# A linear-attention and MLP kernel on one core: a fixed issue order on TensorE, a 5/4 token layout, kv per head, and batches 0 to 2 turned on TensorE

## The chip, the cores and the metric

The kernel runs on one core of a Trainium2 chip. The metric is device time in microseconds (us) of one execution, as the median of several. The profile's span of a run is about 1.7 us shorter than the time that is reported for the same run.

Profile lines name the engines: PE is TensorE (matmuls), PEld its loads of the stationary operand, DVE VectorE, ACT ScalarE, POOL GpSimd, and SP (SPq) SyncE, whose queue issues DMA. L176 is line 176 of that run's kernel. To turn a tile is to transpose it. q turns, kv and o are the small matmuls of the attention; PSUM is the memory that matmuls write to. A hole is a stretch in which TensorE has nothing to run, and a cold matmul one that runs at about half rate.

Executions of the kernel before vary: 342 to 350 us over all chips used here. Some are marked slow: over 1.5% above the fastest of the same kernel on that chip. Ratios below are the mean time of one kernel's fast runs over that of the other's of the same rounds, so not quite the ratio of the medians that are quoted.

## The reference

Eight batches, eight heads, 576 tokens, head width 64. Everything after the attention works on rows of 512 (8 heads of 64).

```python
kv  = einsum('bhsd,bhse->bhde', k, v)              # 64 x 64 per head
out = einsum('bhsd,bhde->bhse', q, kv)
rms = sqrt(mean(out * out, axis=-1) + 1e-6)
x   = (out / rms * g_norm)                          # heads side by side: (8, 576, 512)
xn  = (x - mean(x)) / sqrt(var(x) + 1e-6) * g_ln    # layer norm over 512
res = x + relu(xn @ w_ch1) @ w_ch2                  # 512 -> 2048 -> 512
```

Inputs and output are float32; the kernels load q, k, v and the weights as bfloat16.

## The kernel before

Tokens are taken as 128 partitions of 4 tokens (512), and the other 64 tokens of a batch as a remainder. Two batches' remainders make one tile of 128 rows. So there are 32 main tiles and 4 remainder tiles, and nine MLP blocks of four tiles. MLP 1 is 64 matmuls of 512 columns a block, MLP 2 also 64.

```python
def load_batch(b):                       # casts f32 -> bf16; issued by GpSimd
    for src, main, rem in ((q, q_m, q_r), (k, k_m, k_rem[...]), (v, v_m, v_rem[...])):
        nc.gpsimd.dma_start(main, src[b, :, :S_MAIN, :].rearrange("h (p j) d -> p h j d", j=J))
        nc.gpsimd.dma_start(rem, src[b, :, S_MAIN:, :].rearrange("h p d -> p h d"))

def permuted(b, t, tag):                 # [p, h, j, d] -> [p, j, h, d], for q and for k
    eng = nc.vector if b in PERM_DVE else nc.gpsimd          # PERM_DVE = (0,)
    eng.tensor_copy(t_p.rearrange("p j h d -> p h j d"), t)

def transpose_q(b, q_m, q_r):            # the DMA branch is the one taken for all batches
    q_p = permuted(b, q_m, "qp")
    nc.sync.dma_start_transpose(q_t..., q_p...)
    nc.sync.dma_start_transpose(q_tr, q_r...)

def kv_product(b, k_m, v_m):             # two heads at a time: 128 x 128, 20 matmuls a batch
    k_p = permuted(b, k_m, "kp")
    for hp in range(HP):
        for j in range(J):
            nc.tensor.matmul(kv_ps[:, hp, :], lhsT=k_p[:, j, hs, :]..., rhs=v_m[:, hs, j, :], ...)
        nc.tensor.matmul(...)            # the remainder
    # ... the two diagonal 64 x 64 blocks are copied to kv_pack

def attn_tile(mms, x_blk, mv_blk, xT_blk, ts, xt_pe):
    # o_ps = q_t . kv_pack (4 matmuls); ScalarE: sq, rms; VectorE: ss, inv, y, x, stats, mv,
    xc = work.tile([128, Dm], bf16, tag="xc")                # 3 buffers
    nc.vector.tensor_scalar(xc, x2, mv_blk[:, ts, 0:1], None, op0=ALU.subtract)
    if xt_pe: ...                        # turned on TensorE: batch 0 only
    else:     nc.sync.dma_start_transpose(xT_blk[:, :, ts * 128:(ts + 1) * 128], xc)

# order of issue: attention of batch b+1, then the MLP of batch b
blk0 = attn(0, l0)
for b in range(B):
    if b + 1 < B:
        if b + 2 < B: loads[b + 2] = load_batch(b + 2)
        blks[b + 1] = attn(b + 1, loads.pop(b + 1))
    if b == B - 1: moe(rem_blk, store_rem)
    moe(blks.pop(b), store_main(b))
```

w1 is multiplied by g_ln after it is loaded, by ScalarE and VectorE in turn. The framework's scheduler chooses the order on each engine.

Of the kernel before, what the change touches and what calls it, by code (L numbers as in the profile page):

```python
# [14 lines left out]
def kernel(  # L15
# [11 lines left out]
    nc = tc.nc  # L27
    f32 = mybir.dt.float32
# [8 lines left out]
    assert Dm == 512 and Dh % 512 == 0 and S == 576 and D == 64  # L37
# [3 lines left out]
    J = 4  # L41
    S_MAIN = 128 * J
    S_REM = S - S_MAIN
    EPS = 1e-6
    PERM_DVE = (0,)
    QT_PE = ()
    XT_PE = (0,)

    consts = ctx.enter_context(tc.tile_pool(name="consts", bufs=1))
    kv_in = ctx.enter_context(tc.tile_pool(name="kv_in", bufs=2))  # L50
    qt_pool = ctx.enter_context(tc.tile_pool(name="qt_pool", bufs=2))
# [4 lines left out]
    ps_kv = ctx.enter_context(tc.psum_pool(name="ps_kv", bufs=1))  # L56
    ps_out = ctx.enter_context(tc.psum_pool(name="ps_out", bufs=2))
    ps_tp = ctx.enter_context(tc.psum_pool(name="ps_tp", bufs=1))
    ps1 = ctx.enter_context(tc.psum_pool(name="ps1", bufs=2))
    ps2 = ctx.enter_context(tc.psum_pool(name="ps2", bufs=2))  # L60


    g_norm_sb = consts.tile([128, 1, D], f32)
    nc.scalar.dma_start(
        g_norm_sb,
        bass.AP(tensor=g_norm.tensor, offset=g_norm.offset,
                ap=[[0, 128], [0, 1], list(g_norm.ap[0])]),
    )
    g_ln_col = consts.tile([128, nK, 1], f32)
    g_ln_r = moe_g_ln.rearrange("(ko p) -> p ko", p=128)  # L70
    nc.scalar.dma_start(
        g_ln_col,
        bass.AP(tensor=g_ln_r.tensor, offset=g_ln_r.offset,
                ap=[list(x) for x in g_ln_r.ap] + [[1, 1]]))
    eps_sb = consts.tile([128, 1], f32)
    nc.vector.memset(eps_sb, float(EPS))
    identity = consts.tile([128, 128], bf16)

    w1_sb = consts.tile([128, nK, Dh], bf16)
    w2_sb = consts.tile([128, nDe, Dm], bf16)  # L80

    NB_REM = 2
    k_rem = [consts.tile([128, H, D], bf16, name=f"k_rem{i}") for i in range(NB_REM)]
    v_rem = [consts.tile([128, H, D], bf16, name=f"v_rem{i}") for i in range(NB_REM)]
    kv_pack = [consts.tile([128, HP, 128], bf16, name=f"kv_pack{i}") for i in range(3)]

    def load_batch(b):
        q_m = kv_in.tile([128, H, J, D], bf16, tag="qm")
        k_m = kv_in.tile([128, H, J, D], bf16, tag="km")
        v_m = kv_in.tile([128, H, J, D], bf16, tag="vm")  # L90
        q_r = kv_in.tile([S_REM, H, D], bf16, tag="qr")
        for src, main, rem in ((q, q_m, q_r), (k, k_m, k_rem[b % NB_REM][:S_REM]),
                               (v, v_m, v_rem[b % NB_REM][:S_REM])):
            nc.gpsimd.dma_start(  # L94
                main, src[b, :, :S_MAIN, :].rearrange("h (p j) d -> p h j d", j=J))
            nc.gpsimd.dma_start(
                rem, src[b, :, S_MAIN:, :].rearrange("h p d -> p h d"))
        return q_m, q_r, k_m, v_m

    def load_w1():  # L100
        for c in range(4):
            n = Dh // 4
            sl = slice(c * n, (c + 1) * n)
            nc.gpsimd.dma_start(
                w1_sb[:, :, sl], moe_w_ch1[:, sl].rearrange("(ko p) n -> p ko n", p=128))
            for kk in range(nK):
                if kk % 2 == 0:
                    nc.scalar.mul(w1_sb[:, kk, sl], w1_sb[:, kk, sl], g_ln_col[:, kk, :])  # L108
                else:
                    nc.vector.tensor_scalar(w1_sb[:, kk, sl], w1_sb[:, kk, sl],  # L110
                                            g_ln_col[:, kk, :], None, op0=ALU.mult)

    def load_w2():
        for c in range(4):
            n = nDe // 4
            nc.gpsimd.dma_start(
                w2_sb[:, c * n:(c + 1) * n, :],
                moe_w_ch2[c * n * 128:(c + 1) * n * 128, :].rearrange(
                    "(ko p) n -> p ko n", p=128))

    def permuted(b, t, tag):
        t_p = kv_in.tile([128, J, H, D], bf16, tag=tag)
        eng = nc.vector if b in PERM_DVE else nc.gpsimd
        eng.tensor_copy(t_p.rearrange("p j h d -> p h j d"), t)  # L124
        return t_p

    def transpose_q(b, q_m, q_r):
        q_t = qt_pool.tile([128, J, HP, 128], bf16, tag="qt")
        q_tr = qt_pool.tile([128, HP, S_REM], bf16, tag="qtr", bufs=3)
        q_p = permuted(b, q_m, "qp")  # L130
        if b in QT_PE:
            for j in range(J):
                tp = ps_tp.tile([128, HP, 128], bf16, tag="tp")
                for hp in range(HP):
                    nc.tensor.transpose(tp[:, hp, :], 
                                        q_p[:, j, 2 * hp:2 * hp + 2, :].rearrange("p h d -> p (h d)"),
                                        identity)
                nc.vector.tensor_copy(q_t[:, j], tp)
            tp = ps_tp.tile([128, HP, 128], bf16, tag="tp")
            for hp in range(HP):  # L140
                nc.tensor.transpose(
                    tp[:, hp, :S_REM],
                    q_r[:, 2 * hp:2 * hp + 2, :].rearrange("p h d -> p (h d)"),
                    identity[:S_REM, :S_REM])
            nc.vector.tensor_copy(q_tr, tp[:, :, :S_REM])
        else:
            nc.sync.dma_start_transpose(
                q_t.rearrange("p j hp t -> p (j hp) t"), q_p.rearrange("p j h d -> p (j h d)"))
            nc.sync.dma_start_transpose(q_tr, q_r.rearrange("p h d -> p (h d)"))
        return q_t, q_tr  # L150

    def kv_product(b, k_m, v_m):
        kvp = kv_pack[b % 3]
        k_p = permuted(b, k_m, "kp")
        kv_ps = ps_kv.tile([128, HP, 128], f32, tag="kvps")
        for hp in range(HP):
            hs = slice(2 * hp, 2 * hp + 2)
            for j in range(J):
                nc.tensor.matmul(kv_ps[:, hp, :], lhsT=k_p[:, j, hs, :].rearrange("p h d -> p (h d)"),  # L159
                                 rhs=v_m[:, hs, j, :],  # L160
                                 start=(j == 0), stop=False)
            nc.tensor.matmul(kv_ps[:, hp, :],  # L162
                             lhsT=k_rem[b % NB_REM][:, hs, :].rearrange("p h d -> p (h d)"),
                             rhs=v_rem[b % NB_REM][:, hs, :].rearrange("p h d -> p (h d)"),
                             start=False, stop=True)
        nc.vector.tensor_copy(kvp[:D, :, :D], kv_ps[:D, :, :D])  # L166
        nc.vector.tensor_copy(kvp[D:, :, D:], kv_ps[D:, :, D:])
        return kvp

    def attn_tile(mms, x_blk, mv_blk, xT_blk, ts, xt_pe):  # L170

        o_ps = ps_out.tile([128, H, D], f32, tag="ops")
# [15 lines left out]
        x3 = x_blk[:, ts].rearrange("p (h d) -> p h d", h=H)  # L188
        nc.vector.tensor_mul(x3, y, g_norm_sb.to_broadcast([128, H, D]))  # L189
        x2 = x_blk[:, ts]  # L190
# [3 lines left out]
        xc = work.tile([128, Dm], bf16, tag="xc")  # L194
        nc.vector.tensor_scalar(xc, x2, mv_blk[:, ts, 0:1], None, op0=ALU.subtract)  # L195
        if xt_pe:
            tp = ps_tp.tile([128, HP, 128], bf16, tag="tp")
            for kk in range(nK):
                nc.tensor.transpose(tp[:, kk, :], xc[:, kk * 128:(kk + 1) * 128], identity)  # L199
            nc.vector.tensor_copy(xT_blk[:, :, ts * 128:(ts + 1) * 128], tp)  # L200
        else:
            nc.sync.dma_start_transpose(xT_blk[:, :, ts * 128:(ts + 1) * 128], xc)
# [7 lines left out]
    def rstd_of(blk, lo=0, hi=4):  # L210
        rstd = work.tile([128, 4, 1], f32, tag="rstd")
        nc.scalar.activation(rstd[:, lo:hi], blk[1][:, lo:hi, 1:2], func=AF.Sqrt, bias=eps_sb)
        nc.vector.reciprocal(rstd[:, lo:hi], rstd[:, lo:hi])
        return rstd

    def moe(blk, store):
        x_blk, mv_blk, xT_blk = blk
        rstd = rstd_of(blk)
        m1 = m1pool.tile([128, nDe, 512], bf16, tag="m1")
        for de in range(nDe):  # L220
            p1 = ps1.tile([128, 512], f32, tag="p1")
            for kk in range(nK):
                nc.tensor.matmul(p1, lhsT=w1_sb[:, kk, de * 128:(de + 1) * 128],  # L223
                                 rhs=xT_blk[:, kk, :], start=(kk == 0), stop=(kk == nK - 1))
            nc.scalar.activation(m1[:, de, :], p1, func=AF.Relu)
        for ts in range(4):
            p2 = ps2.tile([128, Dm], f32, tag="p2")
            for de in range(nDe):
                nc.tensor.matmul(p2, lhsT=m1[:, de, ts * 128:(ts + 1) * 128],  # L229
                                 rhs=w2_sb[:, de, :], start=(de == 0), stop=(de == nDe - 1))  # L230
# [88 lines left out]
```

## Time and profile before

Median 348.03 us (346.2 to 349.99, 3 runs). The execution that was profiled took 350.6 us and is marked slow, so the stages and holes below are those of a slow execution; no fast one of this kernel was profiled. The stages are cut at what TensorE does: its first MLP matmul, the end of MLP 1 of batch 0, the first matmul of MLP 1 of batch 2, and its last matmul.

| stage of the kernel before | us |
|---|---|
| start: to the first MLP matmul | 48.30 |
| MLP 1 of batch 0 | 15.76 |
| middle: to the first matmul of MLP 1 of batch 2 | 72.45 |
| rest: to TensorE's last matmul | 207.99 |
| tail | 4.30 |

The busy time of each engine in these stages of the kernel before. In each line the first field is the stretch in us, then its length, then busy us (and instructions) by engine, the clock granted to TensorE as a share of full speed, the DMA share and GB/s:

```profile
core 0: us, PE busy (x) PEld busy (x) DVE busy (x) ACT busy (x) POOL busy (x), PEclk, DMA share, GB/s
0.00:48.30 48.30, 7.09 (x53) 5.23 (x54) 20.88 (x53) 11.24 (x19) 21.14 (x33) 1.00 1.27 172
48.30:64.06 15.76, 15.76 (x64) 6.75 (x64) 0.00 (x0) 8.96 (x15) 5.89 (x5) 1.00 1.54 178
64.06:136.51 72.45, 54.26 (x293) 25.93 (x292) 43.02 (x77) 17.71 (x37) 27.55 (x24) 0.88 1.34 148
136.51:344.50 207.99, 207.76 (x1083) 96.53 (x1080) 96.70 (x205) 84.00 (x164) 15.91 (x15) 1.00 0.36 71
```

TensorE is full in the rest and has room only in the start and the middle. The timeline of TensorE (kernel before) shows where it stood in the middle. Columns: start us, us, engine, line, operation, output and inputs, shapes, count, and in brackets the idle time ahead of it and what ended that:

```profile
start us, us, engine line op out<-in xcount [idle before <-releaser]
70.80 1.03 PE L176 MATMUL o_ps<-kv_pack_105,q_t 128*128 128x128 bf16 x8 [4.16 <-DMA q_t<-t_p]
71.62 4.47 PE L229 MATMUL p_565<-w_sb,m_468 128*128 128x512 bf16 x10
...
89.85 5.27 PE L229 MATMUL p_605<-w_sb,m_468 128*128 128x512 bf16 x16 [8.06 <-DVE o_sb L232]
94.96 3.62 PE L229 MATMUL p_625<-w_sb,m_468 128*128 128x512 bf16 x16
...
101.32 1.02 PE L223 MATMUL p_781<-xT_blk,w_sb 128*128 128x512 bf16 x4 [2.30 <-DMA xT_blk<-xc]
...
126.81 5.30 PE L229 MATMUL p_917<-w_sb,m_780 128*128 128x512 bf16 x16 [3.60 <-DVE o_sb L232]
```

Sixteen matmuls of 512 columns start within 3.46 us (94.96 to the next start at 98.42), 0.216 us each. After three of the four holes (4.16, 8.06 and 3.60 us) the first matmuls take about twice that: 10 in 4.27 us after the first of them. After the hole of 2.30 us they don't: four take 0.86 us.

The same timeline over all engines (kernel before), around the hole of 8.06 us, has a line that the prediction did not read:

```profile
84.08 4.27 DVE L195 TENSOR_SCALAR xc<-x_blk,mv_blk 128x512 bf16<-128x512 f32 x1
84.32 1.91 POOL L124 COPY t_p<-q_m 128x2048 bf16<-128x2048 bf16 x1
86.15 1.91 POOL L124 COPY t_p<-k_m 128x2048 bf16<-128x2048 bf16 x1
```

VectorE's xc took 4.27 us there, against a median of 0.478, and it ended just after two GpSimd copies.

### The profile page before, as it was taken

To read this page: it belongs to the slowest core of one execution; us is meant where nothing else is said; L and a number is where in the kernel's file an instruction comes from. 1 tells how busy PE (TensorE), PEld (TensorE's weight loads), DVE (VectorE), ACT (ScalarE), POOL (GpSimd) and SP (SyncE) were. 2 spreads that over 40 slices of the span, in tenths; PEclk is the share of its full clock that TensorE was granted. 3 is DMA by queue.
4 is the path that set the end of the run, shared out by engine and by line. 5 is a ranking of instruction groups with operands and counts; after the bars stand their busy time and mean duration, and the time that the engine had idled before them with its cause. 6 is when DMAs were issued, how large, how long until landed. Compare 5 with 4: busy or idle time off the path is not lost.

```text
span 348.8 us, 4001 instructions
## 1 busy us (share of the span) xinstructions
PE 284.9 (82%) x1488; PEld 134.4 (39%) x1488; DVE 161.3 (46%) x335; ACT 121.9 (35%) x235; POOL 70.5 (20%) x76
## 2 busy tenths in 40 slices
PE   0021169683679959999999999999999999999994
PEld 0021124342234425444544544454454444444442
DVE  2114940069969123972781397169129820021011
ACT  1013516322037302840670184067018505504600
POOL 8322472455642022220400220000000000000000
PEclk9999999969699989999999999999999999999999
DMA  7999999999999982965851393201220221022011
GB/s 85 177 188 193 198 201 189 136 127 146 149 183 205 171 129 66 143 95 142 107 103 58 88 157 59 90 31 36 57 90 19 58 80 42 0 60 62 0 60 60
DMA packets 84146, 36.98 MB, mean 106 GB/s; under 512 B 50848, under 2 KB 79520, under 8 KB 84128
## 3 DMA queue, kind: packets, MB, share of 16 engines
q0 software_dynamic: 41856, 18.35, 45.3%
q1 hardware_dynamic: 41600, 18.36, 28.2%
q8 instruction: 11, 0.18, 0.2%
q10 hardware_dynamic: 672, 0.03, 0.1%
q14 instruction: 7, 0.06, 0.1%
HBM read 36.73 MB, written 9.44 MB: 132 GB/s over the span
## 4 chain that ended last, share of the span: by engine, by line
PE 64%; DMA 29%; POOL 2%; DVE 1%; issue 1%; SPq 1%; ACT 0%; POOLq 0%; DVEq 0%
DMA q_t<-t_p 9%; DMA k_m<-in_k_dram 6%; DMA q_r<-in_q_dram 5%; DMA v_m<-in_v_dram 4%; DMA xT_blk<-xc 3%; DMA q_tr<-q_r 3%; PE o_ps L176 2%; PE p_917 L229 2%; PE kv_ps L159 1%; PE p_565 L229 1%; PE p_2929 L229 1%; PE p_2889 L229 1%; PE p_2706 L229 1%; PE p_2565 L229 1%; PE p_2505 L229 1%
## 5 line engine op out<-in xcount | busy, mean ns | idle before, releaser
L223 PEld LDWEIGHTS <-w_sb 128*128 128x128 bf16 x576 | 55.5, 98 | 69.3 <-issue 11.0
L195 DVE TENSOR_SCALAR xc<-x_blk,mv_blk 128x512 bf16<-128x512 f32 x36 | 25.6, 711 | 13.7 <-DMA xT_blk<-xc 13.5
L181 DVE TENSOR_REDUCE ss<-sq 128x8 f32<-128x512 f32 x36 | 23.3, 666 | 17.2 <-ACT sq L179 17.2
L179 ACT ACTIVATE sq<-o_ps 128x512 f32<-128x512 f32 x36 | 20.6, 596 | 29.1 <-PE o_ps L176 28.0
L159 PE MATMUL kv_ps<-v_m,t_p 128*128 128x128 bf16 x128 | 11.0, 230 | 18.0 <-DMA v_m<-in_v_dram 18.0
L189 DVE TENSOR_TENSOR x_blk<-y,g_norm_sb 128x512 f32<-128x512 f32 x36 | 25.1, 697 | 0.0
L187 DVE TENSOR_TENSOR y<-o_ps,inv 128x512 f32<-128x512 f32 x36 | 24.7, 686 | 0.8
L192 DVE BATCH_NORM_STATS2 stats<-x_blk 128x6 f32<-128x512 f32 x36 | 24.7, 685 | 0.1
L124 POOL COPY t_p<-q_m 128x2048 bf16<-128x2048 bf16 x7 | 13.4, 1916 | 30.5 <-DMA q_t<-t_p 30.5
L176 PEld LDWEIGHTS <-q_t 128*128 128x128 bf16 x128 | 9.5, 105 | 22.6 <-DMA q_t<-t_p 11.3
L159 PEld LDWEIGHTS <-t_p 128*128 128x128 bf16 x128 | 9.5, 103 | 21.9 <-DVE t_p L124 13.0
L94 POOL DMA_DIRECT2D v_m<-in_v_dram x8 | 7.1, 886 | 53.3 <-PE kv_ps L162 50.0
L183 ACT ACTIVATE rms<-ss,eps_sb 128x8 f32<-128x8 f32 x36 | 10.6, 299 | 10.8 <-DVE ss L181 10.8
L229 PEld LDWEIGHTS <-m_468 128*128 128x128 bf16 x64 | 7.1, 113 | 17.4 <-issue 13.2
L176 PE MATMUL o_ps<-kv_pack_104,q_t 128*128 128x128 bf16 x48 | 5.0, 247 | 10.6 <-DMA q_t<-t_p 6.4
L124 POOL COPY t_p<-k_m 128x2048 bf16<-128x2048 bf16 x7 | 13.4, 1911 | 0.0
L229 PE MATMUL p_605<-w_sb,m_468 128*128 128x512 bf16 x16 | 5.3, 502 | 8.1 <-DVE o_sb L232 8.1
L229 PEld LDWEIGHTS <-m_780 128*128 128x128 bf16 x64 | 6.7, 104 | 12.6 <-issue 6.2
L108 ACT ACTIVATE w_sb<-w_sb,g_ln_col 128x512 bf16<-128x512 bf16 x8 | 5.1, 708 | 17.0 <-DMA w_sb<-in_moe_w_ch_dram 17.0
L199 PE MATMUL tp<-identity,xc 128*128 128x128 bf16 x16 | 2.4, 308 | 10.0 <-DVE xc L195 10.0
L166 DVE CAST kv_pack_105<-kv_ps 64x256 bf16<-64x256 f32 x3 | 1.3, 417 | 18.1 <-PE kv_ps L162 18.1
L229 PEld LDWEIGHTS <-m_1430 128*128 128x128 bf16 x64 | 6.3, 98 | 7.5
(414 smaller groups left out, 529.5 us busy)
## 6 DMA issues: line engine op xcount, KB each, us to landing
out_dram<-o_sb SPq DMA_DIRECT2D x32, 256.0 KB, 2.3
q_m<-in_q_dram POOLq DMA_DIRECT2D x8, 512.0 KB, 15.6
k_m<-in_k_dram POOLq DMA_DIRECT2D x8, 512.0 KB, 16.1
v_m<-in_v_dram POOLq DMA_DIRECT2D x8, 512.0 KB, 10.9
w_sb<-in_moe_w_ch_dram POOLq DMA_DIRECT2D x8, 512.0 KB, 17.1
out_dram<-o_sb SPq DMA_DIRECT2D x8, 128.0 KB, 2.4
q_r<-in_q_dram POOLq DMA_DIRECT2D x8, 64.0 KB, 14.2
xT_blk<-xc SPq DMA_TRANSPOSE x32, 2.5
```

The source lines that it names most:

```text
L124: eng.tensor_copy(t_p.rearrange("p j h d -> p h j d"), t)
L159: nc.tensor.matmul(kv_ps[:, hp, :], lhsT=k_p[:, j, hs, :].rearrange("p h d -> p (h d)"), rhs=v_m[:, hs, j, :], start=(j == 0), stop=False)
L176: nc.tensor.matmul(o_flat[rows, hp * 128:(hp + 1) * 128], lhsT=lhsT_of(hp), rhs=kvp[:, hp, :], start=True, stop=True)
L179: nc.scalar.activation(sq, o_ps, func=AF.Square)
L181: nc.vector.tensor_reduce(ss, sq, axis=AX.X, op=ALU.add)
L183: nc.scalar.activation(rms, ss, func=AF.Sqrt, scale=1.0 / D, bias=eps_sb)
L187: nc.vector.tensor_mul(y, o_ps, inv.to_broadcast([128, H, D]))
L189: nc.vector.tensor_mul(x3, y, g_norm_sb.to_broadcast([128, H, D]))
L192: nc.vector.bn_stats(stats, x2)
L195: nc.vector.tensor_scalar(xc, x2, mv_blk[:, ts, 0:1], None, op0=ALU.subtract)
L223: nc.tensor.matmul(p1, lhsT=w1_sb[:, kk, de * 128:(de + 1) * 128], rhs=xT_blk[:, kk, :], start=(kk == 0), stop=(kk == nK - 1))
L229: nc.tensor.matmul(p2, lhsT=m1[:, de, ts * 128:(ts + 1) * 128], rhs=w2_sb[:, de, :], start=(de == 0), stop=(de == nDe - 1))
```

## The change

The intent is to start the MLP earlier and to keep TensorE fed through batches 1 and 2.

1. TensorE's order is fixed to the order of the program text; all other engines are still scheduled, by priorities set with `due(slot)`. A slot is a group of MLP matmuls of about 0.9 us.
2. Partitions 0 to 63 hold 5 tokens and 64 to 127 hold 4, so one layout holds all 576 tokens and the remainder is a fifth column.
3. kv is computed per head, 40 matmuls of 64x64 a batch, so k needs no permute.
4. q and x of batches 0 to 2 are turned on TensorE, with ScalarE copies; batches 3 to 7 by DMA.
5. MLP 1 of batch 0 runs tile by tile; g_ln is folded into xc instead of w1.

```diff
+    PE_TURN = (0, 1, 2)
+    qt_pool = ctx.enter_context(tc.tile_pool(name="qt_pool", bufs=3))
+    ps1 = ctx.enter_context(tc.psum_pool(name="ps1", bufs=3))
+    ctx.enter_context(tc.manual_schedule(engines={mybir.EngineType.PE}))
+    def due(slot):
+        tc.cur_priority = 100000 + int(slot * 100)
 ...
+    def load_batch(b):                      # k, then v, then q
 ...
+    def turn_q(q_p, q_t, j, n=128):
+        tp = ps_out.tile([128, HP, 128], bf16, tag="ops", name="tp")    # shares o_ps's 2 buffers
+        for hp in range(HP):
+            nc.tensor.transpose(tp[:, hp, :n], q_p[:n, j, 2 * hp:2 * hp + 2, :]..., identity[:n, :n])
+        nc.scalar.copy(q_t[:, j, :, :n], tp[:, :, :n])
+    def turn_q_dma(b):
+        nc.gpsimd.tensor_copy(q_p.rearrange("p j h d -> p h j d"), q_in[b % NB])
+        q_t = qt_pool.tile([128, JJ, HP, 128], bf16, tag="qt")
+        nc.sync.dma_start_transpose(q_t..., q_p...)
+    def kv_of(b):
+        for h in range(H):
+            for j in range(JJ):
+                nc.tensor.matmul(kv_ps[rows, h // 2, :], lhsT=k_in[b % NB][:, h, j, :],
+                                 rhs=v_in[b % NB][:, h, j, :], ...)
 ...
-        nc.vector.tensor_scalar(xc, x2, mv_blk[:, ts, 0:1], None, op0=ALU.subtract)
+        nc.vector.scalar_tensor_tensor(xc, in0=x2, scalar=mv_blk[:, ts, 0:1], in1=g_ln_sb,
+                                       op0=ALU.subtract, op1=ALU.mult)
 ...
+    def rem_tile(b):                        # pops q_t of batches b-1 and b
 ...
+    def q_turns(b):
+        tc.keep_in_program_order(           # pinned behind the VectorE operation traced before it
+            nc.vector.tensor_copy(q_p.rearrange("p j h d -> p h j d"), q_in[b % NB]))
+        for j in range(J):
+            turn_q(q_p, qts[b], j)
+        turn_q(q_p, qts[b], J, 64)
+    PLAN = {1: dict(kv=23, q=23, tiles=[24, 26, 28, 30], turns=[32, 36, 40, 40], rem=48), 3: dict(load=28)}
 ...
+    for ts in range(4):
+        mm1(0, ts, 1)
+    mm2(0, [0, 1], 4)
+    mm2(0, [2, 3], 1)
 ...
```

## The prediction

> **What bounds it now.** The timeline of TensorE splits the 348.8 us in four. (a) 0 to 48.3 us: no MLP matmul; TensorE waits for loads, then for batch 0's VectorE chain. (b) 48.3 to 136.5: MLP with holes. (c) 136.5 to 344.5: TensorE 99.9% busy. (d) 4.3 us of tail. The MLP is 1152 matmuls of 512 columns; 16 take 3.45 us in (c), 0.216 each, 248.8 in all. Small matmuls of batches 1 to 7: about 20 us (a batch of (c) takes 30.5, its MLP 27.6). 48.3 + 248.8 + 20 + 4.3 = 321.4, so about 27 us are holes and cold matmuls in (b): TensorE stood 4.4 us at 66 us (q_t by DMA), 8.1 at 82 and 3.6 at 123 (o_sb late: VectorE waited 13.5 us in all for xc buffers that DMA transposes held), 2.3 at 99 (xT by DMA). After a hole 10 matmuls took 4.27 us, half rate. This agrees with the Trainium skill, "TensorE: Matmul & The Clock Gate", Part 1: an idle window halves the clock.
>
> **What the change does.**
> 1. Start. k isn't permuted; the 128-byte remainder loads go (v's landed 2.8 us after v), and so does the q DMA transpose (8.3 us) beside the loads; the Sqrt table load (1.28 us, in the first chain) comes early; w1 is no longer scaled (7.9 us of ScalarE and VectorE). Above all, MLP 1 starts on tile 0 alone. I estimate v landed at 15 to 16 us, kv at 18, first MLP matmul at 27 (before 48.3). Then tiles come at VectorE's pace: 0.67+0.19+0.69+0.69+0.69+0.18+0.71 = 3.8 us, about 4.1 with gaps, against 64 matmuls of 128 columns at 55 ns warm (four took 0.22 us) = 3.5. So MLP 1 of batch 0 takes about 17 us, not 13.8, and ends near 43 (before 64.1). Gain about 20 us.
> 2. Holes. Batches 1 and 2 no longer wait for DMA transposes; the 27 us mostly go. New ones: five q turns through two PSUM buffers with a ScalarE copy each (2.5 us a batch), and blocking in the fixed order while VectorE holds o_ps. I allow 8.
> 3. Added on TensorE: kv is 40 matmuls of 64x64, not 20 of 128x128 (1.1 us); at 40 to 60 ns each some 6 us in all. Turns of q and x: about 5. Narrow MLP 1 in batch 1: 1.
> 4. (c) and tail: nothing to gain.
>
> **Sum.** 27 + 17 (MLP 1 of batch 0) + 235 (other MLP) + 1 + small 20 + kv 6 + turns 5 - 5 (kv and turns counted in the start) + holes 8 + tail 4.3 = 318; some turns overlap VectorE-bound slack: **316 us**, range **306 to 330**, ratio 0.91. Faster by over 2% 0.95, within 2% 0.03, slower 0.02.
>
> **What would show it.** Timeline: first MLP matmul at 25 to 30 us; MLP 1 of batch 0 ends at 40 to 46. Waits: TensorE's on q_t and xT DMA gone for batches 1 and 2; waits on ScalarE copies and VectorE's y there instead, each under 3 us. From batch 3 on TensorE over 98% busy, 29.5 to 31 us a batch. Chain of waits: TensorE over 80%, loads only in the first 16 us.
>
> **What would make it wrong.** Fixed order stalling: 9 tiles in slots 24 to 50 need about 37 us of VectorE; if it falls behind, TensorE stands behind an o or a turn (to 330). Batch 3's load, permute and DMA transpose may miss their slots. w2's second half, behind batch 1, may land after 47 us. Better: a start at 24 us and 30 ns kv matmuls give 305.

## The result, and the profile after

331.54 us median (331.43 to 332.75, 3 runs), against 348.03; ratio 0.9536 with a 95% interval of 0.9446 to 0.9625. It is faster by over 2%, as forecast, but 1.5 us above the range. The same stages:

| stage | before, us | after, us | difference |
|---|---|---|---|
| start | 48.30 | 27.05 | -21.25 |
| MLP 1 of batch 0 | 15.76 | 17.42 | +1.66 |
| middle | 72.45 | 76.24 | +3.79 |
| rest | 207.99 | 204.69 | -3.30 |
| tail | 4.30 | 4.30 | 0 |

The sum is -19.1 us, which is the difference of the two spans (348.8 and 329.7). It is more than the 16.5 us between the medians, since the profiled execution before was a slow one; part of the differences by stage can be that. The lines of the changed kernel for these stages:

```profile
0.00:27.05 27.05, 6.13 (x76) 5.02 (x77) 10.95 (x29) 7.25 (x16) 14.06 (x25) 1.00 1.12 172
27.05:44.47 17.42, 17.33 (x272) 17.09 (x272) 7.95 (x16) 12.07 (x24) 6.29 (x9) 1.00 1.33 202
44.47:120.71 76.24, 58.60 (x561) 37.54 (x565) 49.64 (x89) 29.97 (x62) 24.64 (x26) 0.89 1.02 149
120.71:325.40 204.69, 201.19 (x1129) 94.69 (x1148) 103.53 (x189) 85.46 (x164) 7.79 (x9) 1.00 0.38 74
```

The start is as predicted. The middle, where some 19 us were to be won, got longer, and its clock is as low as before (0.89 against 0.88).

How much of the middle is holes can be worked out from the traces' own durations. Before: three MLP stages of 64 matmuls at 0.216 us (41.4), three kv at 1.11, eight main tiles of o at 0.22 and a remainder tile: 46.7 us of work, so 25.7 us of holes and cold matmuls. After: two such stages (27.6), MLP 1 of batch 1 in narrow pieces (64 matmuls of 128 columns in 3.57 us, twice, and 64 of 256 at 0.109 us: 14.1), three kv at 0.81, 40 q turns at 0.055, eight x turns and eleven tiles of o at 0.22 and the remainder: 50.8 us of work, so 25.4 us of holes. The change moved the holes; it did not remove them. (A fast execution of the kernel before may have had some us less of them.)

The timeline of TensorE in the changed kernel shows the new ones:

```profile
50.61 0.88 PE L162 MATMUL kv_ps<-v_in,k_in 128*64 128x64 bf16 x40
52.74 0.62 PE L140 MATMUL tp<-identity,q_p 128*128 128x128 bf16 x8 [1.25 <-DVE q_p L326]
...
65.10 1.04 PE L140 MATMUL tp<-identity,q_p 128*128 128x128 bf16 x8 [3.47 <-DVE q_p L326]
...
70.05 2.79 PE L300 MATMUL p<-w_sb,m 128*128 128x512 bf16 x8
...
86.37 0.38 PE L206 MATMUL tp<-identity,xc 128*128 128x128 bf16 x4 [1.60 <-ACT xT_blk L207]
...
95.17 0.42 PE L179 MATMUL o_ps<-kv_pack,qt 128*64 128x128 bf16 x8
...
105.87 0.61 PE L179 MATMUL o_ps<-kv_pack,q_t 128*128 128x128 bf16 x4 [5.82 <-DMA q_t<-q_p]
...
115.94 0.40 PE L206 MATMUL tp<-identity,xc 128*128 128x128 bf16 x4 [1.46 <-DVE xc L196]
```

TensorE no longer waits for DMA in batches 1 and 2. It waits for a VectorE permute before the q turns (1.25 and 3.47 us), and in batch 3 for the DMA transpose of q (5.82 us). After the hole at 65 us, eight matmuls of 512 columns take 2.63 us to the next start (70.05 to 72.68), 0.33 each: still partly cold.

Where the permute of batch 2 stood, in the timeline of all engines (changed kernel):

```profile
62.67 0.38 DVE L166 CAST kv_pack<-kv_ps 64x256 bf16<-64x256 f32 x1
62.98 0.73 DVE L196 SCALAR_TENSOR_TENSOR xc<-x_blk,mv_blk,g_ln_sb 128x512 bf16<-128x512 f32 x1
63.64 0.67 DVE L190 TENSOR_TENSOR y<-o_ps,inv 128x512 f32<-128x512 f32 x1
64.24 0.81 DVE L326 COPY q_p<-q_in 128x2560 bf16<-128x2560 bf16 x1
```

`keep_in_program_order` pins the permute behind the VectorE operation traced last, here the kv_pack copy, and that waits its turn among batch 1's tile chains.

For batch 3, GpSimd finished the permute at 69.55 us (67.22 + 2.33), but the transpose was issued 26 us later. The timeline of the SP queue, which issues the transposes:

```profile
95.73 12.60 SPq L153 DMA_TRANSPOSE q_t<-q_p  x2
```

And the waits of that queue (who waited, for whom, us in total, times, longest):

```profile
SPq L153 <- PE o_ps L179: 22.9, 3, 18.7
```

The transpose waited not for data but for a matmul of o. The turned q has three buffers. Batch 0's is still held when batch 3 wants one, because its fifth column is used by the remainder tile of batches 0 and 1, which stands in slot 48 and ran at 95.17 us (the line with 128*64 above). The transpose could only be issued then, and took until 105.83.

The last hole is VectorE's. The timeline of all engines at 113 us:

```profile
113.02 2.32 POOL L151 COPY q_p<-q_in 128x2560 bf16<-128x2560 bf16 x1 [4.72 <-DMA q_t<-q_p]
113.03 2.85 DVE L196 SCALAR_TENSOR_TENSOR xc<-x_blk,mv_blk,g_ln_sb 128x512 bf16<-128x512 f32 x1
```

xc, 0.75 us in the median, starts beside a GpSimd copy and ends 0.54 us after it. Two other xc took long, 2.34 us at 82.09 and 2.87 at 149.81, and each stood beside such a copy too. The Trainium skill, "SBUF — State Buffer", section "SBUF: two separate sides", says that VectorE and GpSimd share one pair of ports as an exclusive lock held for a whole instruction, and that a VectorE operation with two SBUF inputs, as xc now is, can be the one that stands. These two lines agree with it.

### The profile page after: what moved, and what is told of

Its sections match the earlier page's. It is cut to its first block, busy times and chain, and to the rows that moved or that the text cites. A ratio compares the mean times of both kernels' runs of the same rounds, so it can differ in the third digit from the quotient of the medians.

```text
span 329.7 us, 5123 instructions
## 1 busy us (share of the span) xinstructions
PE 283.2 (86%) x2032; PEld 154.3 (47%) x2060; DVE 172.5 (52%) x322; ACT 134.8 (41%) x265; POOL 52.8 (16%) x69
## 4 chain that ended last, share of the span: by engine, by line
PE 74%; DVE 10%; DMA 6%; ACT 4%; issue 3%; POOL 1%; POOLq 0%; DVEq 0%; SPq 0%; ACTq 0%
PE p L268 35%; PE p L300 34%; DMA v_in<-in_v_dram 3%; DMA q_t<-q_p 3%; DVE xc L196 2%; PE o_ps L179 2%; PE kv_ps L162 2%; DVE x_blk L191 1%; DVE ss L184 1%; DVE y L190 1%; DVE o_sb L304 1%; ACT xT_blk L207 1%; DVE stats L193 1%; ACT qt L144 1%; ACT m L271 1%
## 5 line engine op out<-in xcount | busy, mean ns | idle before, releaser
L268 PE MATMUL p<-xT_blk,w_sb 128*128 128x512 bf16 (+2 forms) x887 | 130.7, 306 | 4.6 <-ACT xT_blk L207 2.3
L300 PE MATMUL p<-w_sb,m 128*128 128x512 bf16 x557 | 131.8, 388 | 1.6 <-issue 0.8
L271 ACT ACTIVATE m<-p 128x512 bf16<-128x512 f32 x144 | 84.1, 594 | 43.9 <-PE p L268 42.9
L268 PEld LDWEIGHTS <-w_sb 128*128 128x128 bf16 x896 | 73.4, 100 | 56.2 <-issue 5.2
L300 PEld LDWEIGHTS <-m 128*128 128x128 bf16 x576 | 55.9, 100 | 64.3 <-issue 3.9
L304 DVE SCALAR_TENSOR_TENSOR o_sb<-p,rstd,x_blk 128x512 f32<-128x512 f32 x36 | 26.9, 746 | 91.6 <-PE p L300 79.6
L196 DVE SCALAR_TENSOR_TENSOR xc<-x_blk,mv_blk,g_ln_sb 128x512 bf16<-128x512 f32 x36 | 32.8, 911 | 0.9
L151 POOL COPY q_p<-q_in 128x2560 bf16<-128x2560 bf16 x5 | 11.6, 2325 | 36.1 <-DMA q_t<-q_p 22.5
L179 PE MATMUL o_ps<-kv_pack,q_t 128*128 128x128 bf16 (+1 forms) x100 | 9.2, 224 | 5.9 <-DMA q_t<-q_p 5.8
L144 ACT COPY qt<-tp 128x512 bf16<-128x512 bf16 (+1 forms) x15 | 7.5, 545 | 13.6 <-PE tp L140 13.6
```

The source lines that it names most:

```text
L179: nc.tensor.matmul(o_flat[rows, hp * 128:(hp + 1) * 128], lhsT=lhsT_of(hp), rhs=kvp[:, hp, :], start=True, stop=True)
L196: nc.vector.scalar_tensor_tensor(xc, in0=x2, scalar=mv_blk[:, ts, 0:1], in1=g_ln_sb, op0=ALU.subtract, op1=ALU.mult)
L268: nc.tensor.matmul(p1[:, i, :], lhsT=w1_sb[:, kk, de * 128:(de + 1) * 128], rhs=blk[2][:, kk, sl], start=(kk == 0), stop=(kk == nK - 1))
L271: nc.scalar.activation(m1[:, de0:de0 + per, sl], p1, func=AF.Relu)
L300: nc.tensor.matmul(p2s[ts], lhsT=m1[:, de, ts * 128:(ts + 1) * 128], rhs=w2_sb[:, de, :], start=(de == 0), stop=(de == nDe - 1))
L304: nc.vector.scalar_tensor_tensor(o_sb, in0=p2s[ts], scalar=rstds.pop((b, ts))[:, ts], in1=blks[b][0][:, ts], op0=ALU.mult, op1=ALU.add)
```

## The experiments

Eleven kernels ran, and e10 is the fastest of them. All gave correct results. Each set ran beside the kernel before on its own chip (347.9, 347.9 and 348.5 us). In the first two sets four of the seven runs of the kernel before are marked slow, and the record calls every comparison with it there unclear, e13's as well; e12 and e14 are called faster. The experiments are therefore compared with one another and with the change. The comparisons with the change (331.54 us) cross chips; differences under 2 us between sets are not read.

### e1: one more buffer for turned q

```diff
-    qt_pool = ctx.enter_context(tc.tile_pool(name="qt_pool", bufs=3))
+    qt_pool = ctx.enter_context(tc.tile_pool(name="qt_pool", bufs=4))
```

> One buffer more for turned q (4, was 3); the order on TensorE, VectorE and ScalarE is unchanged. Theory A (the DMA transpose of batch 3's q waits for the buffer of batch 0's q, which the remainder tile in slot 48 frees at 95.2 us): the transpose starts soon after its permute, before 85 us, TensorE's 5.8 us wait for q_t goes, its cold matmuls after it too; 6 to 9 us less, 323 to 326 us. Rival B (load, permute or the transpose itself is late, or the queue is): the transpose still starts near 95 us or lands near 105, and the time stays at 330 to 333.

324.03 us median (320.67 to 325.66, 5 runs, one marked slow). By fast runs alone the median is 323.66. The orders of operations on TensorE, VectorE and ScalarE are the same as in the change; on the SP queue this transpose comes earlier, and on GpSimd a permute and loads moved with it. The SP queue's timeline (e1):

```profile
67.60 4.66 SPq L153 DMA_TRANSPOSE q_t<-q_p  x1
```

The transpose is issued 28 us earlier, at once after its permute. TensorE's wait for q_t is gone, and the middle shrinks by 9.8 us in the trace (43.79 to 110.26, 66.47 us). The buffer was the cause of that hole, worth 7.5 us by the medians.

### e2: the VectorE permutes of q earlier

```diff
+        if pe:
+            at({1: 16, 2: 23}[b], lambda b=b: q_perm(b))      # were in slots 23 and 27
         at(p.get("q", ...), lambda b=b: q_turns(b) ...)       # q_turns now only turns
```

> The VectorE permutes of q of batches 1 and 2 are moved earlier in the order (slots 16 and 23, were 23 and 27). Theory A (TensorE stood 1.25 and 3.47 us at the q turns only because the permute stood behind other VectorE work whose inputs came late): both waits shrink below 0.5 us, and 3 to 6 us of the time go, 326 to 329 us. Rival B (VectorE's tile chain of batches 1 and 2 is the limit, about 4 us a tile): the waits turn up again at the x turns of batch 1 or at the q_t hole, and less than 1.5 us go.

327.84 us median (326.98 to 328.55, 4 runs), 3.7 less, inside A's band. The wait of batch 1 is gone. Batch 2's is partly replaced: VectorE now stands 3.49 us for q of batch 2, which lands only at 54.7 us, and TensorE waits 1.74 and 0.89 us for ScalarE copies between the turns. So A holds in the time, and in the waits only for batch 1; for batch 2, moving the permute alone runs into the load.

### e3: TensorE scheduled like the other engines

```diff
-    ctx.enter_context(tc.manual_schedule(engines={mybir.EngineType.PE}))
```

> The line that fixes TensorE's order is taken out; everything else of the change stays, and the scheduler orders TensorE by the due slots as it does the other engines. Theory A (the holes come from when inputs are ready, not from the fixed order): the time doesn't improve, 329 to 345 us. Rival B (the loss is TensorE standing behind one late operand while other work is ready): faster than 328 us.

331.68 us median (331.3 to 332.04, 4 runs): no difference in all. The trace shows two that cancel. MLP 1 of batch 2 starts 5.2 us earlier than in the change (115.48 against 120.71), so TensorE standing in a fixed order did cost time in the middle. From there to its last matmul, TensorE takes about 5 us longer (209.8 against 204.7), with the pattern of lone matmuls that is shown under e12. The fixed order thus lost about 5 us in the middle of the change and won about 5 in the rest. Timeline of TensorE (e3):

```profile
115.48 9.66 PE L267 MATMUL p<-xT_blk,w_sb 128*128 128x512 bf16 x43 [0.56 <-ACT xT_blk L206]
```

(The scheduler orders the other engines anew as well when this line goes; it is not TensorE's order alone that differs.)

### e4: MLP 1 of batch 0 on all four tiles at once

```diff
-    for ts in range(4):
-        mm1(0, ts, 1)
+    mm1(0, 0, 4)          # and all four x turns of batch 0 ahead of it
```

> MLP 1 of batch 0 waits for all four tiles again (512 columns) instead of starting on tile 0 alone. Theory A (the start by tiles is worth what it saves until MLP 1 of batch 0 ends): first MLP matmul at 39 to 42 us, MLP 1 of batch 0 ends at 54 to 56 (was 44.5), and the time is 337 to 343. Rival B (the holes of batches 1 and 2 hang on loads and VectorE, so an earlier end of MLP 1 is given back there): under 4 us more.

336.26 us median (334.79 to 340.69, 4 runs, one marked slow), 4.7 us more: between the two theories. The first MLP matmul came at 36.24 us, earlier than expected, because four tiles were ready sooner; MLP 1 then took 15.0 us, as expected, and ended at 51.2. Of 6.7 us at that point 3.4 were given back by the start of MLP 1 of batch 2 (124.07 us against 120.71). So starting on tile 0 is worth 9.2 us at the first matmul, 6.7 at the end of MLP 1 and 5 in the time. The other 12.9 us by which MLP 1 ends earlier than in the kernel before (64.06 to 51.2) come from loads, kv and chain together, which no run takes apart.

### e7: e1 with the GpSimd permute in five pieces

```diff
-        nc.gpsimd.tensor_copy(q_p.rearrange("p j h d -> p h j d"), q_in[b % NB])
+        for j in range(JJ):
+            nc.gpsimd.tensor_copy(q_p[:, j], q_in[b % NB][:, :, j, :])
```

> As e1 (four buffers of turned q), and the GpSimd permute of q for batches 3 to 7 is five copies of a fifth instead of one of 2.32 us. Theory A (VectorE's xc, which reads two SBUF tensors, stands for as long as a GpSimd copy runs: 2.34 and 2.85 us instead of 0.75): no xc takes over 1.5 us, TensorE's wait for xc in batch 3 (1.8 us in e1) falls under 0.8, and the time is 0.5 to 3 us under e1's, 321 to 323.5. Rival B (xc is long for another reason, or the wait moves): some xc still over 2 us, or the time within 0.5 us of e1's.

320.4 us median (319.46 to 321.39, 4 runs). No xc takes over 1.09 us, as A says, and VectorE's operations get in between the five copies (timeline of all engines, e7):

```profile
103.31 3.76 POOL L152 COPY q_p<-q_in 128x512 bf16<-128x512 bf16 x5 [2.38 <-DMA q_in<-in_q_dram]
103.95 1.08 DVE L192 TENSOR_TENSOR x_blk<-y,g_norm_sb 128x512 f32<-128x512 f32 x1
104.95 1.09 DVE L197 SCALAR_TENSOR_TENSOR xc<-x_blk,mv_blk,g_ln_sb 128x512 bf16<-128x512 f32 x1
```

But TensorE's wait for xc in batch 3 stayed (1.96 us), which A had at under 0.8, and the profiled runs of e1 and e7 took about the same (320.67 and 321.39). e1 ran on another chip. Alone, e7 does not settle the worth; e9 and e10 do.

### e9: batches 1 and 2 retimed

```diff
 def load_batch(b):
+    load(q_in[b % NB], q, b)               # q first, was last
     load(k_in[b % NB], k, b)
     load(v_in[b % NB], v, b)
-    load(q_in[b % NB], q, b)
-    PLAN = {1: dict(kv=23, q=23, tiles=[24, 26, 28, 30], turns=[32, 36, 40, 40], rem=48), 3: dict(load=28)}
+    PLAN = {1: dict(kv=16, tiles=[18, 20, 23, 26], turns=[31, 35, 38, 39], rem=48), 3: dict(load=20)}
+    # q permutes in slots 10 and 19; q turns one to a slot: 12, 13, 14, 15, 15 and 27 to 31
+    # and four buffers of turned q, as in e1
```

> As e1, and batches 1 and 2 are retimed: q is loaded ahead of k and v; the q permutes are issued earlier; the five q turns of a batch go one to a slot instead of all in one; kv of batch 1 in slot 16 (was 23) and its tiles in 18, 20, 23, 26; its x turns one or two slots before the matmuls that read them. Theory A (the rest of the holes between 44 and 110 us, 12 to 15 us beside the q_t wait, come from where these few operations stand in the orders, not from VectorE's throughput): TensorE's waits after 27 us fall under 5 us in all and the time is 310 to 317. Rival B (VectorE's 4 us a tile, or the loads, bound this stage): the waits turn up at the x turns of batch 1 or at the q turns of batch 2, and the time is 319 to 325.

316.56 us median (313.29 to 317.63, 4 runs), 7.5 under e1 and inside A's band. A's other half failed: TensorE's waits after 27 us are 7.6 us in all, not under 5, and one of 2.54 us stands at a q turn of batch 2, as B said. Another hole is larger than before: 3.50 us for xc of batch 3. Timeline of all engines (e9):

```profile
60.73 0.40 PE L140 MATMUL tp<-identity,q_p 128*128 128x128 bf16 x4 [2.54 <-DVE y L190]
...
94.68 2.32 POOL L151 COPY q_p<-q_in 128x2560 bf16<-128x2560 bf16 x1 [2.15 <-DMA q_in<-in_q_dram]
95.13 2.41 DVE L191 TENSOR_TENSOR x_blk<-y,g_norm_sb 128x512 f32<-128x512 f32 x1
...
100.78 0.61 PE L206 MATMUL tp<-identity,xc 128*128 128x128 bf16 x4 [3.50 <-DVE xc L196]
```

VectorE's multiply of two SBUF tensors stands for the GpSimd copy, the chain behind it is late, TensorE stands 3.5 us, and its next 20 matmuls take 6.8 us (101.18 to 107.97) instead of 4.3: eleven of them are cold, at 0.43 us.

### e10: e9 with the GpSimd permute in pieces

The edit is that of e7 on top of e9.

> e9 with the GpSimd permute in five pieces as in e7. If the two causes are separate, it is 0.5 to 3 us under e9; if e9 has slack on VectorE, the two are the same within 0.5 us.

310.6 us median (310.31 to 311.74, 4 runs), 6.0 under e9 on the same chip: more than the sum expected. In the profiled run TensorE does not go cold any more (mean clock 1.00; the other three runs had 0.991 to 0.994, and e9's four 0.982 to 0.995). e9's fastest run, at 0.995, took 313.29 us, and e10's three at 0.991 to 0.994 took 310.31 to 311.74: about half of the 6 us is there at the same clock, and the rest goes with the lower clock of e9's other runs. The ratio to the kernel before is 0.9034 (0.8944 to 0.9124), and it is 6% under the change. The stages of e10:

```profile
0.00:27.06 27.06, 6.14 (x77) 5.02 (x78) 10.95 (x29) 7.26 (x16) 14.05 (x25) 1.00 1.11 172
27.06:45.30 18.24, 17.82 (x293) 17.32 (x292) 8.68 (x17) 14.24 (x29) 7.20 (x10) 1.00 1.33 202
45.30:101.50 56.20, 51.05 (x545) 33.59 (x545) 45.41 (x88) 27.32 (x57) 27.36 (x41) 1.00 1.35 173
101.50:304.40 202.90, 202.55 (x1152) 94.65 (x1148) 101.65 (x189) 85.67 (x164) 8.81 (x13) 1.00 0.43 81
```

The middle is 56.2 us, 20 us less than in the change, at full clock. The work in it, counted as above (the q turns of batch 1 now lie in the stage ahead), is 49.7 us, so 6.5 us of holes are left, within the 8 that the prediction had allowed.

### e11: batch 2 turned by DMA, on top of e1

```diff
-    PE_TURN = (0, 1, 2)
+    PE_TURN = (0, 1)                       # q, kv and tiles of batch 2 in slots 20, 26, 32 to 50
```

> As e1, but batch 2 is turned by DMA like batches 3 to 7, in the same slots: TensorE loses 5 q turns and 4 x turns, ScalarE 9 copies, VectorE a permute. Theory A (turning batch 2 on TensorE costs more holes than it saves, as the q turns of batch 2 stood 5 to 6 us around 62 us): 318 to 322 us. Rival B (q of batch 2 lands at about 55 us, so permute on GpSimd and DMA transpose come too late, as in the kernel before): TensorE waits over 3 us for q_t or xT of batch 2, and the time is 324 to 332.

339.24 us median (338.33 to 340.31, 4 runs), 15 us over e1. Rival B is right in kind and was too mild. TensorE waits 7.2 us for q_t and, in one piece, 16.8 us for xT of batch 2 (timeline of TensorE, e11):

```profile
128.48 1.86 PE L268 MATMUL p<-xT_blk,w_sb 128*128 128x512 bf16 x4 [16.82 <-DMA xT_blk<-xc]
```

The SP queue issues transposes and stores in one order, so the x transposes of batch 2 also queue behind later batches' q transposes (issued at 99.97 and 107.53 us, ahead of x transposes at 104.92 and 113.34) and behind stores. The x transpose that TensorE waited for was issued 7.9 us after its xc was ready (109.42 to 117.27) and landed 11.1 us later (128.39). Turning batch 2 on TensorE was right, and is worth about 15 us against this set of slots; other slots for the DMA form were not tried.

### e12: e10 without the fixed order

The edit is that of e3 on top of e10.

> e10 without the line that fixes TensorE's order, as e3 was to the change. Theory A (the slots and buffers do the work, not the fixed order, as e3 and the change took the same time): within 3 us of e10's 310.6. Rival B (the fixed order is worth something once no operand comes late): slower than e10 by over 5 us, 316 or more.

325.96 us median (324.69 to 328.32, 4 runs), 15 us over e10. Rival B holds: a fixed order that was worth nothing net in e3 is worth 15 us once the late operands are gone. The slots were set for that order, and without it the scheduler places the other engines' work differently too, so these 15 us are those of the order and all that follows it. In the trace the middle is 7.2 us longer (MLP 1 of batch 2 starts at 108.74, not 101.51), which was not taken apart, and the last stage 6.7 us (209.6 instead of 202.9, to 318.3). The last stage grew because the scheduler puts kv and the o matmuls of the remainder tiles one by one between MLP matmuls. Timeline of TensorE (e12, an early such place):

```profile
48.69 0.22 PE L162 MATMUL kv_ps<-v_in,k_in 128*64 128x64 bf16 x1
48.84 0.39 PE L300 MATMUL p<-w_sb,m 128*128 128x512 bf16 x1
49.16 0.22 PE L162 MATMUL kv_ps<-v_in,k_in 128*64 128x64 bf16 x1
49.31 0.39 PE L300 MATMUL p<-w_sb,m 128*128 128x512 bf16 x1
```

Such a lone kv matmul and one MLP matmul take 0.47 us together (48.84 to 49.31); in e10, with kv in blocks of 40, the two take 0.216 and 0.02. A lone matmul of a remainder tile (128*64) costs 0.22 us more than in e10's blocks of eight, a lone o matmul of a main tile (128*128) nothing. e12's last stage has 15 more such places for kv than e10's and 15 for remainder tiles: an estimate of 15 x 0.23 + 15 x 0.22 = 6.8 us, against the 6.7 measured.

### e13: the kernel before with its GpSimd permutes in pieces

```diff
-        eng.tensor_copy(t_p.rearrange("p j h d -> p h j d"), t)
+        for j in range(J):                                    # on GpSimd; VectorE as before
+            eng.tensor_copy(t_p[:, j], t[:, :, j, :])
```

> The kernel before, with its GpSimd permutes of q and k (1.91 us each, two in a row) in four pieces each. Theory A (VectorE's xc of 4.27 and 4.19 us at 84 and 94 us stood for the two copies, and with it o_sb and TensorE's hole of 8.1 us): no xc over 1.5 us, that hole shrinks by 3 us or more, and the time falls by 3 to 8 us, 340 to 345. Rival B (the holes of the kernel before are DMA transposes alone, as the prediction said): xc gets shorter, but the time stays within 2 us of 348.

343.11 us median (342.47 to 349.36, 4 runs, one marked slow), 5.4 us less than the kernel before in the same set; by fast runs the ratio is 0.9846 (0.9789 to 0.9903), which the record calls unclear. The time is in A's band, but the kernel before ran 342 to 343 us without any edit in four of 14 executions on the other two chips, so the edit is not shown to have won the 5.4 us. A's reason is refuted. The hole stayed (8.26 us), and so did xc (timeline of all engines, e13):

```profile
81.92 4.35 DVE L199 TENSOR_SCALAR xc<-x_blk,mv_blk 128x512 bf16<-128x512 f32 x1
82.04 2.29 POOL L128 COPY t_p<-q_m 128x512 bf16<-128x512 bf16 x4
84.26 2.47 POOL L128 COPY t_p<-k_m 128x512 bf16<-128x512 bf16 x4
...
89.68 3.37 DVE L193 TENSOR_TENSOR x_blk<-y,g_norm_sb 128x512 f32<-128x512 f32 x1
```

xc, here with one SBUF tensor, stood through nearly all eight copies, though they are separate instructions. At 89.68 us x_blk, a multiply of two SBUF tensors, stood 3.37 us through most of the next eight; in e7 the same kind of multiply took 1.08 us beside five. So the number of VectorE's SBUF inputs is not what differs; what does is not settled, and neither is where the 5.4 us came from: the order on TensorE also changed in this build (kv now lies between MLP matmuls).

### e14: kv twice, on top of e10

```diff
-        for h in range(H):
+        for h in [h for h in range(H) for _ in range(2)]:
```

> e10 with every 64x64 matmul of kv done twice (the second overwrites the first; the result is right). If a kv of 40 takes 0.88 us, as the timeline shows, and lies on the critical path, 7 us are added, 317 to 319. If it cost what the prediction took, 40 to 60 ns a matmul, 13 to 19 us; if it hid in holes, under 3.

321.04 us median (318.74 to 325.59, 4 runs, one marked slow), 10.4 over e10, or 9.2 by fast runs alone (319.83): above the 7 us that the first theory gave, below the 13 to 19 of the prediction's figure. In the trace, kv of batch 1 went from 0.81 us (45.28 to 46.09) to 1.95 (46.10 to 48.05), so 1.14 more a batch and 9.1 for eight, close to the 9.2. Timelines of TensorE, e10 and then e14:

```profile
45.28 0.88 PE L163 MATMUL kv_ps<-v_in,k_in 128*64 128x64 bf16 x40
...
46.10 2.02 PE L163 MATMUL kv_ps<-v_in,k_in 128*64 128x64 bf16 x80
```

A hole of 2.62 us for a ScalarE result at 108 us is new. kv lies on the critical path, and one pass costs 0.8 us. The doubled one costs more than twice that, 24 ns a matmul instead of 20. The starts of the single matmuls in the traces show how: in e10 two matmuls, one to each half of the columns, start 5 ns apart and the next pair 27 ns later, 32 ns a pair. Where only one half has work, one matmul starts every 32 ns; with ten in a row to one half, e14 has many of these.

Left open: kv two heads at a time in the new layout, so what kv per head is worth against the old form is not known.

## Why the prediction was right or wrong

- **Start (step 1): right.** First MLP matmul predicted at 27, measured 27.05; MLP 1 of batch 0 to end near 43, measured 44.47. The gain of about 20 us was 19.6 at that point (64.06 to 44.47). That MLP 1 took about 17 us (17.42) is luck, though: the prediction had its tiles come at VectorE's pace, 4.1 us each, but TensorE was busy 17.33 of the 17.42 us and VectorE 7.95. What made it long was other work of TensorE in between and a slow beginning: the first 48 matmuls of 128 columns took 4.50 us, where 48 at 55.8 ns are 2.68.
- **Holes (step 2): wrong, and this is the step that failed.** The prediction said "the 27 us mostly go" and "I allow 8". The cause it named did go: TensorE does not wait for DMA in batches 1 and 2. But the waits did not go with it: the next-latest operands took their place, and holes and cold matmuls in the middle were 25.4 us against 25.7 in the (slow) profile before. 17 us were missing from the sum there. The runs show in what:
  - one buffer too few for turned q, held by a remainder tile in slot 48: 7.5 us (e1). The prediction named batch 3's "load, permute and DMA transpose" as a risk; all were in time, and the buffer wasn't looked at, though the pool's three buffers and the slot stood in the diff;
  - the VectorE permute pinned behind the kv copy: 3.7 us (e2), and with the rest of the retiming 7.5 us beyond e1 (e9);
  - VectorE standing for GpSimd copies: 6.0 us in the retimed version (e9 to e10).

  Together, 331.54 to 310.6 (on two chips), they give back 20.9 us; the middle of the trace gives 20.0.
- **"Waits ... each under 3 us": wrong** (3.47 and 5.82 us). That matters twice, because TensorE ran cold after these two. The clock was 0.89 in the middle of the change and 1.00 in e10, whose longest wait after its start is 2.0 us. This agrees in kind with the Trainium skill, "TensorE: Matmul & The Clock Gate", Part 1, where an idle window of about 3.4 us halves the clock. The length of a single hole does not settle it, though: in e9 a half-rate stretch followed a hole of 2.54 us, and in the change one came at 54.8 us, after the q turns of batch 1, with no hole over 1.25 us.
- **kv (step 3): mis-sized, in the other direction.** 40 to 60 ns a matmul and 6 us more were predicted. Measured: 20 ns, 0.81 us a batch against 1.11, so about 2.4 us less in eight batches, a term 8 us too high. Without this the prediction would have been further off.
- **Stage (c) (step 4): nearly right.** TensorE was busy 98.3% of the rest, and batches 3 to 5 took 29.4 to 31.4 us. About 3 us of holes there were not foreseen.
- With these three terms the sum of 318 becomes 318 + 17 - 8 + 3 = 330, and the span was 329.7. The other terms fit as a sum; they were not checked one by one.
- **The chain of waits: wrong.** TensorE had 74% of it, not over 80%, and the transpose of q for batch 3 had 3%, which is the hole.
- **The reading of the kernel before was incomplete.** It put the late o_sb down to xc buffers held by DMA transposes (13.5 us of waits, right as far as it goes) and did not see that xc itself took 4.27 us beside GpSimd copies. e13 did not settle what that is worth.
- **The fixed order** is the headline of the change. The prediction has it only as a danger, its blocking within the 8 us of step 2 and "Fixed order stalling" among what would make it wrong, and gives it no gain. It is worth nothing net in the change (e3: about 5 us lost in the middle, 5 won in the rest) and 15 us in e10 (e12).

## What to carry to other kernels

When a schedule is fixed, go through every pool of buffers and ask which late, small consumer holds the oldest one: here a remainder tile kept a buffer for 26 us after the next tile wanted it (69.55 to 95.2), and one more buffer of 5 KB a partition gave 7.5 us. When a change removes one wait, don't credit the whole hole; list what else has to be ready at that point, on every engine, since in an in-order stream the next-latest operand sets the new hole. Finally, test an enabling feature again after the other obstacles are gone: the fixed order showed no net effect until they were, and only the trace by stages showed that a loss hid a gain.

## What the Trainium skill lacked or had wrong

- "TensorE: Matmul & The Clock Gate", section "Back-to-back issue gap", gives 81 ns for matmuls of 128 columns and 131 ns for 512 in a stream with weight loads. The runs show 55.8 ns (64 in 3.57 us) and 216 ns (16 in 3.46 us), which is what the page gives for the isolated gap.
- The same page, section "Wait — 56ns, not 53.3ns?", gives about 25 ns as the least distance of two matmuls, without the exception of matmuls in different parts of the array, which the page's Part 3 has about 4 ns apart. Forty 64x64 matmuls whose outputs alternate, by head, between the two halves of the partitions took 0.81 us to the next operation's start, 20 ns each: in pairs that start 5 ns apart, one pair every 32 ns. With ten instead of five in a row to one half they took 24 ns each (e14).
- "SBUF — State Buffer", section "SBUF: two separate sides", says that the pair of ports is locked for one instruction. It doesn't say what happens with several GpSimd instructions in a row: a VectorE operation stood 4.35 us through nearly all of eight copies of about 0.6 us (e13), while in e7 another stood no longer than 1.09 us in all.
- No page read says what it costs when stores and DMA transposes are issued in one order from one queue. In e11 an x transpose stood 7.9 us in it and took 11.1 us to land, and TensorE waited 16.8 us for it.
